# Gated linear attention into a gated state-space block: two of ten moves per group become ScalarE copies, and one group's moves change places with loads in the queue

## The chip, the cores and the metric

The kernel runs on one core of a Trainium2 chip. The metric is the device time of one execution in microseconds. A second number, the span, is the time from the first to the last instruction that the hardware profiler recorded in one profiled execution; the execution's own time is a little longer than its span.

## The reference

Batch B = 4, heads H = 8, sequence S = 768, head size D = 48; the model width is H·D = 384, and the inner width of the second block is 512. All arrays are fp32 (two weights arrive in double precision and are converted on the chip).

```python
# first block, per batch and head
for t in range(S):
    state = alpha[t, :, None] * state + outer(k[t], v[t])     # D x D
    y[t] = q[t] @ state
# bridge: (B,H,S,D) -> (B,S,H*D)
x = y.transpose(0, 2, 1, 3).reshape(B, S, H * D)
# second block
val, gate = split(x @ w_in)                                    # 2 x 512 wide
for t in range(S):
    h = exp(A_log) * h + val[t]
    ys[t] = h
out = (silu(gate) * ys) @ w_out
```

## The kernel before, in words

Two programs stand in the kernel; `fast` runs, and `general` only if a check at the end finds inputs outside of what `fast` can treat. All that follows is `fast`.

**Tiling.** The work is cut into N = 12 groups of 256 time steps (three groups a batch), each of G = 2 chunks of C = 128. The first block runs in its chunked form: a running product of alpha scales q and k, `scores` makes 128 x 128 score tiles, `masks` keeps the causal half, `values` multiplies by v, `state` and `carried` bring in what came before the chunk. The result of a group is in two PSUM tiles `y[0]` and `y[1]`, each 128 x 2 x 256. Head h = 4s + 2e + i lies in tile i, column block e, on partitions 64s to 64s + 47; time runs along the free axis. So a head has its 48 channels on the partitions 0 to 47 or 64 to 111.

**The bridge.** The second block wants x transposed, xT: 384 channels on the partitions as three blocks (kk = 0, 1, 2) of 128, time along the free axis. Head h occupies the channels 48h to 48h + 47. `join` evicts `y[1]` and `y[0]` with one ScalarE activation each (lines 727 and 728) into `y_sb`, and then `transfers` moves each head with a DMA from `y_sb` to its rows of xT (line 738); heads 2 and 5 cross a border of two blocks and take two moves, so that a group takes ten. Heads 0 and 4 go to the rows 0 of block 0 and 64 of block 1, which are also the partitions that they come from.

**The second block.** `project(n, cc)` makes for each cc of NI = 4 blocks of 128 inner channels the two products pv and pg (line 754), kk = 0, 1, 2 in turn for each, from xT and the weights. `hidden` runs the recurrence as a scan on VectorE (line 762); `gate` takes Silu of pg on ScalarE (line 773) and multiplies on GpSimd (line 774); in group 0 it multiplies on VectorE (line 770), with Silu at line 906. `output` multiplies by w_out (line 787) and stores.

**Weights.** They come as double precision bit patterns and are put together by `low_word` (ScalarE, line 512), `high_word` (VectorE, lines 526 and 528) and `word_sum` (GpSimd, line 535), in between the first groups' work. The first pv of group 0 needs the first of these sums.

**Order.** The program runs under a manual schedule: each engine executes its instructions in the order in which the code writes them, and the framework adds only the waits. SP issues almost all DMAs in one queue. Completion semaphores of DMAs are reused in turn, eight for SP's and eight for GpSimd's: a DMA's issue waits until the one eight earlier of that kind has landed. Groups 0, 1 and 2 load alpha, k and q in natural layout (`pair`, line 421) and transpose them on TensorE (`natural_alpha`, line 577; `natural_qk`, line 596); from group 3 on they come in another layout (`loads`, line 406) and VectorE transposes them (line 619). The start of the program is written out by hand. There, group 0's moves are issued by GpSimd, and all later groups' by SP:

```python
    join(0, nc.gpsimd)()
    ...
    join(1, SP)()
    load_v(2, SP)
    for cc in range(NI):
        pv, pg = project(0, cc)
```

In SP's queue the loads of alpha, k and q of group 2 stand after the weights, then the ten moves of group 1, then v of group 2, then the loads of group 3. From group 2 on, the block for n in 1..N-1 interleaves group n's second block with group n + 1's first; its `attend` ends with `join(m, SP)()`, and the next round's `block(n, 0)` reads that xT.

Of the kernel before, what the change touches and what calls it, by code (L numbers as in the profile page):

```python
# [13 lines left out]
AF = mybir.ActivationFunctionType  # L14
# [332 lines left out]
def fast(  # L347
# [18 lines left out]
    nc = tc.nc  # L366
    B, H, S, D = q.shape
    DM = H * D
    DI = moe_A_log.shape[0]
    C = 128  # L370
# [47 lines left out]
    def load_natural(name, m, c, engine):  # L418
        b, g = divmod(m, NG)
        src = {"a": alpha, "q": q, "k": k}[name]  # L420
        engine.dma_start(out=natural(name, m)[:, c, :, 0:D],  # L421
                         in_=src[b, :, ds(g * GC + c * C, C), :].rearrange("h p d -> p h d"))
# [4 lines left out]
    def load_v(m, engine, cs=range(G)):  # L427
        b, g = divmod(m, NG)
        for c in cs:
            engine.dma_start(out=vs[m % NV][:, c, :, 0:D],  # L430
                             in_=v[b, :, ds(g * GC + c * C, C), :].rearrange("h p d -> p h d"))
# [14 lines left out]
    def load_w_out(i, engine):  # L446
        engine.dma_start(out=bits_out[:, ds(2 * i, 2)].rearrange("p cc n two -> p cc (n two)"),
                         in_=moe_w_out.bitcast(U32)[ds(2 * C * i, 2 * C)].rearrange("(cc p) n -> p cc n", p=C))
# [251 lines left out]
    def carried(m, c):  # L700
        ch = (m % NG) * G + c
        if not ch:
            return
        for e in range(2):
            for s in range(2):
                for i in range(2):
                    p, rows = 2 * s + e, ds(64 * i, D)
                    nc.tensor.matmul(ys[m][i][ds(64 * s, D), e, ds(c * C, C)], S_sbs[ch - 1][rows, p, :],  # L708
                                     Zs[m][rows, p, 0, ds(c * C, C)], start=False, stop=True,
                                     skip_group_check=True)  # L710
# [12 lines left out]
    def join(m, engine):  # L723

        y = ys.pop(m)
        y_sb = p2.tile([C, 4, GC], FP32, tag="y_sb", name="y_sb")
        nc.scalar.activation(y_sb[:, 1::2], y[1], AF.Copy)
        nc.scalar.activation(y_sb[:, 0::2], y[0], AF.Copy)
        xT = xTs[m] = p2.tile([C, NK, GC], FP32, tag="xT", name="xT")

        def transfers():
            for h in range(H):
                s, a = divmod(h, 4)
                d = 0
                while d < D:
                    kk, row = divmod(h * D + d, C)
                    size = min(D - d, C - row)
                    engine.dma_start(out=xT[ds(row, size), kk], in_=y_sb[ds(64 * s + d, size), a])  # L738
                    d += size
        return transfers  # L740
# [54 lines left out]
    SP, ACT = nc.sync, nc.scalar  # L795
# [5 lines left out]
    def pair(name, m, one, other):  # L801
        load_natural(name, m, 0, one)
        load_natural(name, m, 1, other)
# [31 lines left out]
    k_times, q_times = natural_qk(0, "k"), natural_qk(0, "q")  # L835
    for i in range(2):
        load_w_out(i, SP)
    for name in "akq":
        pair(name, 2, SP, SP)

    warm(2)
    evict = natural_alpha(1)
# [21 lines left out]
    state(0, 1)  # L864
    carried(0, 1)
    join(0, nc.gpsimd)()
    k_times, q_times = natural_qk(1, "k"), natural_qk(1, "q", ps_mm)
    warm(2)
# [30 lines left out]
    carried(1, 0)  # L899
    carried(1, 1)  # L900
    join(1, SP)()
    load_v(2, SP)
    for cc in range(NI):
        pv, pg = project(0, cc)
# [15 lines left out]
    for n in range(1, N):  # L920
# [8 lines left out]
        def attend():  # L929
            if att:  # L930
                state(m, 0)
                values(m, 0)
                values(m, 1)
                state(m, 1)
                carried(m, 0)
                carried(m, 1)
                join(m, SP)()
# [49 lines left out]
@with_exitstack  # L987
def kernel(ctx: ExitStack, tc: tile.TileContext, *args):
    with tc.manual_schedule():
        good = fast(tc, *args)  # L990
    with tc.If(good <= 0):
        general(tc, *args)
# [30 lines left out]
```

## Time and profile before

| | us |
|---|---|
| median of 4 runs | 304.48 (302.75 to 305.66) |
| the profiled execution's own time | 303.63 |
| its span | 301.9 |
| TensorE busy (PE) | 287.3 |
| TensorE weight loads (PEld), beside PE | 227.2 |
| VectorE busy (DVE) | 226.2 |
| GpSimd busy (POOL) | 106.8 |
| ScalarE busy (ACT) | 95.1 |
| DMA, mean rate over the span | 143 GB/s |

The profile is one execution. Engines run side by side, so their busy times don't add up to the span. A releaser, written after an arrow, is what ended an idle time, inferred from semaphores. "SPq" is SP issuing a DMA, and the time of such a row covers the issue, with any holding back by full queues, not the transfer; a chain entry "DMA xT<-y_sb" is from issue to landing. Times written as moments are from the span's start.

### The profile page before, as it was taken

The page shows a single profiled execution, that of the slowest core. Times are in us where ns is not written, and L with a number is a line of the kernel's source. Part 1 is how long each engine was busy: PE and PEld are TensorE (multiplying, and loading weights), DVE is VectorE, ACT ScalarE, POOL GpSimd, SP SyncE. Part 2 cuts the span into 40 slices and gives each one's busy share as a digit, 9 for nine tenths or more (in the row PEclk, how much of TensorE's full clock was granted, in tenths as well). Part 3 has the DMA queues.
Part 4 walks back from the last instruction along what each step waited for, and adds up shares of the span by engine and source line. Part 5 has one row for each costly group of instructions (what it writes and reads, how often), then busy time and mean ns, then how long its engine had stood idle before and what let it go on. Part 6 is the DMA issues. An engine that isn't in the chain of part 4 may idle for free.

```text
span 301.9 us, 6124 instructions
## 1 busy us (share of the span) xinstructions
PE 287.3 (95%) x2347; PEld 227.2 (75%) x2347; DVE 226.2 (75%) x263; ACT 95.1 (32%) x198; POOL 106.8 (35%) x107
## 2 busy tenths in 40 slices
PE   7899699999999999999999999999999999999990
PEld 3497486887687787787887887886886886885860
DVE  5999398789899399699699699699699695302200
ACT  4264234151521521421531521521531531321111
POOL 6035843053352243262333333452423523411110
PEclk9999889999999999999999999999999999999998
DMA  9999995999398694695693595793693401101101
GB/s 131 163 191 322 321 148 108 230 269 201 105 237 133 166 230 70 166 224 83 182 219 67 140 226 86 189 210 67 179 216 66 106 9 46 52 21 35 52 7 59
DMA packets 72782, 43.26 MB, mean 143 GB/s; under 512 B 47876, under 2 KB 72104, under 8 KB 72744
## 3 DMA queue, kind: packets, MB, share of 16 engines
q1 hardware_dynamic: 71376, 42.19, 68.4%
q8 instruction: 20, 0.33, 0.5%
q0 software_dynamic: 320, 0.39, 0.5%
q10 hardware_dynamic: 1048, 0.20, 0.4%
q14 instruction: 18, 0.15, 0.2%
HBM read 33.33 MB, written 4.72 MB: 126 GB/s over the span
## 4 chain that ended last, share of the span: by engine, by line
PE 86%; DMA 7%; SPq 3%; ACT 1%; issue 1%; ACTq 0%
PE pv L754 22%; PE pg L754 21%; PE o L787 19%; PE sc L674 7%; PE y L697 7%; DMA xT<-y_sb 5%; PE st L718 3%; PE y L708 3%; PE tp L664 2%; DMA raw_q<-in_q_dram 2%; SPq L738 2%; SPq L421 1%; PE warm L823 1%; PE tn L596 1%; PE tn L577 1%
## 5 line engine op out<-in xcount | busy, mean ns | idle before, releaser
L774 POOL TENSOR_TENSOR f<-sg,hh 128x256 f32<-128x256 f32 x44 | 57.1, 1298 | 104.7 <-ACT sg L773 65.3
L754 PE MATMUL pv<-xT,w_in 128*128 128x256 f32 x288 | 73.4, 390 | 3.2 <-DMA xT<-y_sb 3.2
L754 PE MATMUL pg<-xT,w_in 128*128 128x256 f32 x288 | 71.2, 384 | 0.0
L787 PE MATMUL o<-w_out,f 128*128 128x384 f32 x192 | 64.1, 487 | 0.0
L754 PEld LDWEIGHTS pv<-xT,w_in 128*128 128x128 f32 x288 | 53.0, 191 | 14.1 <-issue 3.5
L754 PEld LDWEIGHTS pg<-xT,w_in 128*128 128x128 f32 x288 | 55.5, 193 | 8.2 <-DVE hh L762 0.5
L787 PEld LDWEIGHTS o<-w_out,f 128*128 128x128 f32 x192 | 36.4, 190 | 22.9 <-DVE hh L762 0.2
L685 POOL TENSOR_TENSOR A<-A,mask 128x512 f32<-128x512 f32 x22 | 27.5, 1271 | 67.0 <-ACT A L684 67.0
L773 ACT ACTIVATE sg<-pg 128x256 f32<-128x256 f32 x44 | 16.9, 383 | 93.7 <-PE pg L754 93.7
L762 DVE TENSOR_TENSOR_SCAN hh<-a_dec,hh,pv 128x256 f32<-128x256 f32 x32 | 23.3, 728 | 27.1 <-PE pv L754 25.2
L628 DVE TENSOR_TENSOR_SCAN prod<-aT,first 128x1024 f32<-128x1024 f32 x12 | 32.4, 2700 | 0.1
L640 DVE TENSOR_TENSOR_SCAN inv<-aT,last 128x1025 f32<-128x1025 f32 x12 | 30.1, 2507 | 0.4
L686 DVE TENSOR_TENSOR A<-sc,mask 128x512 f32<-128x512 f32 x22 | 15.0, 689 | 19.4 <-PE sc L674 19.3
L791 ACT ACTIVATE o_sb<-o 128x384 f32<-128x384 f32 x24 | 11.8, 490 | 50.8 <-PE o L787 46.5
L674 PEld LDWEIGHTS sc<-Z 48*128 48x128 f32 x384 | 22.4, 188 | 3.2 <-issue 2.4
L674 PE MATMUL sc<-Z 48*128 48x128 f32 x384 | 24.7, 279 | 0.0
L697 PE MATMUL y<-A,v 128*64 128x128 f32 x384 | 23.5, 274 | 0.0
L697 PEld LDWEIGHTS y<-A,v 128*64 128x64 f32 x384 | 20.7, 137 | 0.4 <-DVE A L686 0.3
L619 DVE STREAM_TRANSPOSE aT<-raw_a 128x1024 f32<-128x1024 f32 x9 | 18.4, 2040 | 0.0
L619 DVE STREAM_TRANSPOSE Z<-raw_q 128x1024 f32<-128x1024 f32 x9 | 18.2, 2022 | 0.0
L619 DVE STREAM_TRANSPOSE Z<-raw_k 128x1024 f32<-128x1024 f32 x9 | 18.2, 2020 | 0.0
L762 DVE TENSOR_TENSOR_SCAN hh<-a_dec,pv 128x256 f32<-128x256 f32 x16 | 10.7, 667 | 7.2 <-PE pv L754 7.2
(93 smaller groups left out, 262.8 us busy)
## 6 DMA issues: line engine op xcount, KB each, us to landing
raw_k<-in_k_dram SPq DMA_DIRECT2D x24, 192.0 KB, 5.5
raw_q<-in_q_dram SPq DMA_DIRECT2D x24, 192.0 KB, 6.3
v<-in_v_dram SPq DMA_DIRECT2D x24, 192.0 KB, 6.6
out_dram<-o_sb SPq DMA_DIRECT2D x24, 192.0 KB, 1.9
raw_a<-in_alpha_dram SPq DMA_DIRECT2D x23, 192.0 KB, 4.1
xT<-y_sb SPq DMA_DIRECT2D x66, 48.0 KB, 2.0
raw_a<-in_alpha_dram SPq DMA_DIRECT2D x18, 176.0 KB, 4.2
raw_k<-in_k_dram SPq DMA_DIRECT2D x18, 176.0 KB, 5.8
```

The lines of the kernel that those rows point to most:

```text
L619: nc.vector.transpose(out=to.rearrange("p h (c j) -> p h j c", j=NT), in_=raw_bufs[m % NR][name].rearrange("p h (j d) -> p h j d", d=D)[:, ...
L628: nc.vector.tensor_tensor_scan(out=prod, data0=aT[:, 0:4 * GC], data1=first.rearrange("p h n -> p (h n)"), initial=0.0, op0=ALU.mult, op1= ...
L640: nc.vector.tensor_tensor_scan(out=inv[:, ::-1], data0=aT[:, ::-1], data1=last.rearrange("p h n -> p (h n)")[:, 0:4 * GC + 1][:, ::-1], in ...
L674: nc.tensor.matmul(sc[i][:, p, :], Z[rows, p, 1, cols], Z[rows, p, 0, cols], start=True, stop=True)
L685: nc.gpsimd.tensor_mul(A[:, 1], A[:, 1], mb)
L686: nc.vector.tensor_mul(A[:, 0], sc[0], mb)
L697: nc.tensor.matmul(ys[m][i][ds(64 * s, 64), e, ds(c * C, C)], v_sb[:, c, 2 * p + i, :], A[:, i, p, :], start=(c == 0 and e == 0), stop=Fal ...
L754: nc.tensor.matmul(pj, w_in[cc][:, kk, vg, :], xT[:, kk, :], start=(kk == 0), stop=(kk == NK - 1))
L762: nc.vector.tensor_tensor_scan(out=hh, data0=a_dec[:, cc:cc + 1].to_broadcast([C, GC]), data1=pv, initial=prev_h[cc][:, GC - 1:GC] if n % ...
L773: nc.scalar.activation(sg, pg, AF.Silu)
L774: nc.gpsimd.tensor_mul(fs[n][:, cc, :], sg, hh)
L787: nc.tensor.matmul(os[c], fs[n][:, cc, ds(c * C, C)], w_out[:, cc, :], start=(cc == 0), stop=(cc == NI - 1))
```

## The change

`join` no longer copies all of y[0] to `y_sb`. It copies the half that holds heads 2 and 6, and writes heads 0 and 4 with two ScalarE activations of 48 x 256 from PSUM straight to their rows of xT; the moves are then eight. The order on ScalarE is: y[1] to `y_sb`, half of y[0] to `y_sb`, head 0, head 4. Each move waits only for the eviction that it reads, so the first one of a group (head 1 now) waits for y[1] alone. Apart from that, the four loads of k and q of group 2 leave their place ahead of group 1's moves in SP's queue and stand behind them.

```diff
@@ join
         nc.scalar.activation(y_sb[:, 1::2], y[1], AF.Copy)
-        nc.scalar.activation(y_sb[:, 0::2], y[0], AF.Copy)
+        nc.scalar.activation(y_sb[:, 2], y[0][:, 1], AF.Copy)
         xT = xTs[m] = p2.tile([C, NK, GC], FP32, tag="xT", name="xT")
 
         def transfers():
             for h in range(H):
                 s, a = divmod(h, 4)
+                if not a:
+                    kk, row = divmod(h * D, C)
+                    nc.scalar.activation(xT[ds(row, D), kk], y[0][ds(64 * s, D), 0], AF.Copy)
+                    continue
                 d = 0
                 while d < D:
...
     for i in range(2):
         load_w_out(i, SP)
-    for name in "akq":
-        pair(name, 2, SP, SP)
+    pair("a", 2, SP, SP)
...
     join(1, SP)()
+    for name in "kq":
+        pair(name, 2, SP, SP)
     load_v(2, SP)
```

GpSimd's instructions lose two moves in group 0 and keep their order otherwise; SP's lose two moves in each of the eleven later groups; TensorE's and VectorE's are the same, in the same order.

## The prediction

> **What bounds the kernel now.** I read the engines' shares first, then the chain that ended last, then the timeline wherever the chain leaves the tensor engine.
>
> ```profile
> PE 287.3 (95%) x2347; PEld 227.2 (75%) x2347; DVE 226.2 (75%) x263; ACT 95.1 (32%) x198; POOL 106.8 (35%) x107
> PE 86%; DMA 7%; SPq 3%; ACT 1%; issue 1%; ACTq 0%
> L754 PE MATMUL pv<-xT,w_in 128*128 128x256 f32 x288 | 73.4, 390 | 3.2 <-DMA xT<-y_sb 3.2
> ```
>
> TensorE is busy 95% of the span and carries 86% of the chain. From 96 us on the chain is TensorE and next to nothing else, some 22.3 us a group, so a gain of the tensor engine before that point stays to the end, and what is not TensorE's lies in front of it. Its only row with real idle time is pv (line 754), 3.2 us, all of it for the moves into xT. The chain in order of time shows where:
>
> ```profile
> 21.84 0.60 ACT y_sb L727
> 22.43 0.50 ACT y_sb L728
> 22.94 0.30 issue
> 23.23 6.75 DMA xT<-y_sb
> 29.98 0.28 issue
> 30.26 5.91 DMA xT<-y_sb
> 36.17 0.45 issue
> 36.62 1.19 PE pv L754 x2
> 37.82 2.25 PE pg L754 x6
> ...
> 78.69 3.32 DMA xT<-y_sb
> ```
>
> Columns are start, length, what. The chain passes through two xT moves of group 0 in a row, one released by the other. The timeline tells why, and what else hangs there:
>
> ```profile
> 30.26 1.02 POOL L738 DMA_DIRECT2D xT<-y_sb  x2 [2.62 <-DMA xT<-y_sb]
> 47.61 0.42 PEld L577 LDWEIGHTS tn<-ident,raw_a 128*128 128x128 f32 x4 [0.18 <-DVE f L770]
> 70.96 8.32 SPq L738 DMA_DIRECT2D xT<-y_sb  x10
> 82.15 0.67 PE L754 MATMUL pv<-xT,w_in 128*128 128x256 f32 x2 [0.52 <-DMA xT<-y_sb]
> ```
>
> GpSimd issues eight moves from 23.23 to 27.64 and then sits 2.62 us until the first has landed: moves nine and ten (heads 6 and 7) reuse the completion semaphores of the first two. They go out at 30.26 and 30.77 and land 5.9 and 5.8 us later, the last at 36.53; the eighth went out at 27.12 and landed 6.6 us later, at 33.70. The second place is group 2: pv begins at 80.50 and its last two matmuls wait until 82.15.
>
> ```profile
> 32.80:36.20 3.40, 1.11 (x4) 0.34 (x3) 0.50 (x1) 1.61 (x3) 3.40 (x5) 1.00 1.03 361
> 36.20:39.60 3.40, 2.98 (x7) 2.47 (x8) 1.71 (x4) 0.00 (x0) 0.84 (x1) 0.50 1.04 183
> 45.00:50.00 5.00, 5.00 (x26) 3.79 (x25) 3.81 (x11) 3.18 (x6) 2.87 (x3) 1.00 0.21 53
> 50.00:58.00 8.00, 8.00 (x39) 5.93 (x38) 6.30 (x6) 1.84 (x5) 0.67 (x1) 1.00 1.07 217
> ```
>
> Here the columns after the length are busy time of PE, PEld, DVE, ACT, POOL, then granted clock, DMA share, GB/s. TensorE has 1.11 us of work in 3.4 us while it waits, and runs the next 3.4 us at half clock. The DMA engines are nearly idle from 45 to 50 us and full (1.07 to 1.10) from 50 to 76.
>
> **What the skill says.** "TensorE: Matmul & The Clock Gate", Part 1 on the HAM clock gate: the clock is halved after an idle window of about 3.4 us, in free-running windows of 3413 ns. The trace agrees in length: half clock from 36.20 for 3.4 us. "DMA: Bandwidth & Descriptors", Queues, rings and completion order: each DMA engine takes turns, packet by packet, between the queues that have work for it. A POOL move takes 6.6 us beside the weight loads where an SP move in a quiet stretch takes 2.0, so the small moves share but do not overtake. "ScalarE: Activation LUTs", What ACT_TABLE_LOAD costs: an ACTIVATE with immediate operands takes 186 ns + 0.833 ns an element, less 93 ns back to back. For 512 elements that is an estimate of 0.61; the trace has 0.60.
>
> **Part one: eight moves a group, two ACT copies.**
>
> 1. ACT. Before: two evictions of 512 columns, 21.84 to 22.93. After: one of 512, then three of 256 (half of y0, heads 0 and 4). The 128x256 ACTIVATE of line 773 takes 383 ns, so about 0.3 each back to back: 0.60 + 0.9 = 1.5, that is 0.4 more a group. After the join ACT's next work in group 0 is line 512 at 24.77, which waits for a load: hidden by 1.4 us. In group 3 the evictions end at 91.28 and the next Silu (line 773) waits for pg until 92.99: hidden by 1.7. Cost nothing; with that cover gone 11 groups by 0.4, 4.4 us.
> 2. POOL's start. Its first move is now head 1, which needs only y1, done at 22.44, so it starts at about 22.74 instead of 23.23: 0.5 earlier.
> 3. POOL's end. Eight moves carry the same bytes as the first eight before, and no move waits for a landing. Issue ends at about 27.2, and the last lands at 33.70 - 0.5 = 33.2. Were the landing time set by the full DMA engines alone it would stay at 33.7; both ends are kept.
> 4. The weight sums of line 535 stand behind the moves on POOL: from 31.29 to about 27.2. Their inputs are there (DVE done 26.53, ACT 25.70). The first pv waits for nothing else.
> 5. TensorE. carried(1,1) still ends near 32.6. pv's kk = 0 and 1 take 4 x 0.215 = 0.86 (1.29 us for six), so kk = 2 starts at 33.46, after the landing at 33.2. Before it started at 36.62: 3.16 earlier (2.8 with the late bound).
> 6. Clock. The wait that emptied the window before 36.2 is gone, so it should stay full. pv's last two and pg took 1.19 + 2.25 = 3.44 where full clock takes 0.43 + 1.29 = 1.72: 1.72 more. Together 4.88 at the end of pg.
> 7. What is late next: DVE in that loop. Per block it does scan 0.68, four weight operations of 0.55, product 0.41, so 3.3 us against TensorE's 2.59. Before, first scan to third product ran 37.85 to 47.55 with 0.42 idle, so 9.28 of work. After: 33.95 + 9.28 = 43.23. The transposes tn at 47.61 already waited for it, and now go at 43.35 where TensorE alone would give 43.0. So 4.25 us arrive at 48, not 4.88.
>
> **Part two: k and q of group 2 behind xT of group 1 on SP.** SP waits before each transfer for the landing of the one eight earlier, and also for room: the second raw_a of group 2 is issued from 28.09 to 35.02. Then:
>
> 8. The eight xT(1) moves start at about 35.1 (y1 is ready at 33.93). The last two wait for the raw_a landings (39.62, 40.50), so they end at about 41.2 and land at about 43. TensorE reads xT(1) at 54.24 - 4.25 = 50.0. With ten moves in the old place the last lands near 50.8, with eight there about 49; so this step by itself frees little.
> 9. The four k and q transfers move from 35.12 to about 41.3. In an empty queue v takes 3.6 us from issue to landing and raw_a 4.9; I take 4.0: first k at 45.3, then 1.2 us each as before, the last q at 48.9. The transposes of line 596 need it at 56.83 - 4.25 = 52.6. Hidden with 3.7 us to spare.
> 10. Then v(2), and group 3's loads. Before, the hole in DMA lasted from q's landing at 45.05 to v's at 52.49; now there is a shorter one from 40.5 to 45.3. The v loads land at 50.1 and 51.3, the first raw_a of group 3 at 52.1 instead of 54.98: the full stream runs 2.9 us earlier. Bounds: 0 if the new hole is as long as the old, 4 if no hole is left.
> 11. xT(2), at the end of that stream. Before, the first move was held by full queues until 73.58 and the others followed at 0.63. The eighth was issued at 77.43; less 2.9 this is 74.5, and with 2.0 to 3.3 us to land 76.5 to 77.8. TensorE wants it at 80.50 + 0.86 - 4.25 = 77.1. I take 77.3. Gain at that point 82.15 - 77.3 = 4.8.
> 12. Later groups: the last xT(3) move lands at 101.58 and is read from 103.5, so moves saved there are worth nothing.
>
> Sum: 4.8 us off the profiled execution, whose own time is 303.63 (span 301.9 and 1.7 around it): 298.8. The median of the four runs is 0.85 higher, 304.48, which gives 299.7. The clock's windows run free, and in other runs the same wait may empty two of them, so I put it at 299.5.
>
> **Rivals.**
> - A, the forecast: 299.5, of which gains between 3.1 and 7 us count.
> - B, the full DMA stretch takes it back. For it: DMA share 1.07 to 1.10 from 50 to 76, and xT(2) stands behind v(3). If step 10 brings nothing, xT(2) is only 1.26 earlier by its two moves, pv's kk = 2 starts at 80.9, and the gain is 1.3 us: 303.2; with half of step 10, 301.7. Against it: the DMA share of 0.21 between 45 and 50. I take 302.5.
> - C, slower: k and q of group 2 come too late. They now wait behind eight moves which wait for the slowest loads (raw_a took 12.4 us to land). Each us after 52.6 is one us of TensorE; the gain is gone when q lands after 57.4, which is 8.5 us past my estimate. A landing at 61.5 gives 304.5 - 4.8 + 8.9 = 308.6. Against it: from 41 us the queue is empty, and nothing in the trace takes 16 us from issue to landing.
> - D, the copies don't spare the wait because something else holds pv: then step 7's DVE loop or ACT's copies decide, and the time stays near 304. Against it: in step 4 every input is there by 29.2.
>
> **Numbers.** A 0.72, B 0.17, C 0.05, D 0.06. A measurement of this kernel can tell about 1% (3.0 us) from no change. A is faster by over 1%, and a third of B's spread comes over that line too, which I count as 0.04. Faster 0.76, same 0.19, slower 0.05. The range takes in the late bounds of steps 10 and 11 and half of B at the top, and a second half-clock window in the median run at the bottom: 297.4 to 302.4.
>
> **What would show it.** Right: POOL's moves without a wait and its line-535 sums at 27; pv without a pause after 33.5 and no half clock after 36; tn (line 577) near 43.4; k and q landed by 49; xT(2)'s last move at 77 to 78. Wrong: pv's last pair waiting beyond 34.5 (step 3), line 596 waiting for raw_k or raw_q (step 9), pv of group 2 waiting until 79 or more (step 10).

## The result and the profile after

The changed kernel has a median of 302.41 us (37 runs, 299.7 to 305.85) against 303.64 for the kernel before (58 runs): ratio 0.9937, 95% interval 0.992 to 0.9954. The medians are of all runs; the ratios, here and below, leave out runs more than 1.5% above the fastest of the same kernel, among them one of 1033.66 us of the fix without the change. That is about 1.9 us by the ratio (1.2 by the medians), where 5.0 were forecast (299.5, range 297.4 to 302.4, against a median of 304.48). The profiled execution took 302.82, with a span of 301.1.

The page's shares, the chain's and the row of pv, which was TensorE's only one with real idle time before:

```profile
PE 287.3 (95%) x2347; PEld 227.0 (75%) x2347; DVE 226.2 (75%) x263; ACT 100.4 (33%) x222; POOL 104.5 (35%) x105
PE 87%; DVE 4%; SPq 3%; DMA 2%; issue 1%; ACT 1%; ACTq 0%
L758 PE MATMUL pv<-xT,w_in 128*128 128x256 f32 x288 | 73.2, 389 | 3.3 <-DMA xT<-y_sb 3.3
```

The wait for xT did not go: 3.3 us, as before 3.2. It has moved. The timeline of the start (columns: start, length, engine, line, what, count, idle time before and its releaser):

```profile
22.71 4.22 POOL L742 DMA_DIRECT2D xT<-y_sb  x8 [2.83 <-ACT y_sb L728]
26.99 1.97 POOL L535 TENSOR_TENSOR w_in<-w_in,wr 128x384 int32<-128x384 int32 x2
32.51 1.56 PE L758 MATMUL pv<-xT,w_in 128*128 128x256 f32 x6
43.35 0.42 PEld L577 LDWEIGHTS tn<-ident,raw_a 128*128 128x128 f32 x4 [0.52 <-DVE f L774]
```

GpSimd issues eight moves without a stop, the weight sums follow at 26.99, the first pv runs all six matmuls through, and tn (the transposes of group 2's alpha) starts at 43.35, where before it was 47.61. `block(1, 0)` starts at 49.97 instead of 54.24: TensorE is 4.27 us ahead. The same view from 65 us on, around the moves of group 2:

```profile
65.58 0.60 ACT L727 ACTIVATE y_sb<-y 128x512 f32<-128x512 f32 x1 [2.50 <-PE y L708]
70.31 9.13 SPq L742 DMA_DIRECT2D xT<-y_sb  x8
77.72 0.67 PE L758 MATMUL pv<-xT,w_in 128*128 128x256 f32 x2 [1.43 <-DMA xT<-y_sb]
78.92 0.67 PE L758 MATMUL pv<-xT,w_in 128*128 128x256 f32 x2 [0.52 <-DMA xT<-y_sb]
80.97 1.19 PE L758 MATMUL pv<-xT,w_in 128*128 128x256 f32 x2 [1.38 <-DMA xT<-y_sb]
```

All three pairs of group 2's pv wait, 3.33 us together, and the last goes at 80.97, only 1.18 ahead of before (82.15). SP needs 9.13 us for eight moves, where ten took 8.32. It also comes to them late. The first eviction of group 2's y ends at 66.2, and SP issues the first move at 70.31. The transfer eight earlier in SP's order, whose completion semaphore that move takes over, is the third load of k of group 4; it landed at 70.23. So a wait of the kind that the change removes from GpSimd's moves now stands in front of SP's. In the kernel before, y was evicted only at 70.94, and its first move went at 70.96. The busy times by stretch show the rest (after the length: PE, PEld, DVE, ACT, POOL, then granted clock, DMA share, GB/s):

```profile
41.00:45.00 4.00, 3.89 (x21) 2.80 (x20) 3.25 (x7) 2.08 (x5) 2.21 (x3) 1.00 0.38 84
45.00:50.00 5.00, 5.00 (x17) 3.01 (x16) 4.46 (x6) 1.70 (x4) 0.00 (x0) 1.00 1.10 161
76.90:80.50 3.60, 1.34 (x4) 0.59 (x4) 0.76 (x2) 0.26 (x1) 2.34 (x2) 1.00 0.22 55
80.50:83.90 3.40, 2.93 (x7) 2.42 (x8) 1.70 (x2) 0.00 (x0) 0.00 (x0) 0.51 0.93 263
```

The half clock that stood at 36.2 to 39.6 now stands at 80.5 to 83.9, after a window with 1.34 us of TensorE work in 3.6; in the chain the last pair and pg take 1.19 + 2.25 = 3.44 us where before they took 0.67 + 1.29 = 1.96. At pg's end the changed kernel stands at 84.41, the kernel before at 84.11. So in these two executions the whole gain is given back in one place: from 4.27 ahead to 1.18 ahead by waiting, 3.09 us, and from there to 0.30 behind by the clock, 1.48. The 1.9 us are an average over executions: those of the changed kernel with a mean granted clock of 0.996 or more took 299.7 to 301.4 us, those at 0.990 to 0.993 mostly 301.8 to 303.5, so half clock in the middle of the program seems not to come in every one. Where it falls in each is not shown. After that both run the same, and TensorE's last product is done 0.3 us later than before. The span is nevertheless 0.8 shorter, because the issue of the last store took SP 0.33 instead of 1.52; nothing in the change accounts for that.

The DMA hole lies at 41 to 45 us now (share 0.38), where it was at 45 to 50 (0.21). The loads of group 3 begin to land at 53.85 (54.98 before), and v of group 3, right ahead of group 2's moves in the queue, lands at 76.13 (76.30 before).

### The profile page after: what moved, and what is told of

Same layout as the page of the kernel before. It is cut to its first block, busy times and chain, and to the rows that moved or that the text cites. A ratio compares the mean times of both kernels' runs of the same rounds, so it can differ in the third digit from the quotient of the medians.

```text
span 301.1 us, 6112 instructions
## 1 busy us (share of the span) xinstructions
PE 287.3 (95%) x2347; PEld 227.0 (75%) x2347; DVE 226.2 (75%) x263; ACT 100.4 (33%) x222; POOL 104.5 (35%) x105
## 4 chain that ended last, share of the span: by engine, by line
PE 87%; DVE 4%; SPq 3%; DMA 2%; issue 1%; ACT 1%; ACTq 0%
PE o L791 21%; PE pv L758 21%; PE pg L758 19%; PE y L697 7%; PE sc L674 7%; PE st L718 4%; PE y L708 3%; PE tp L664 2%; DMA raw_q<-in_q_dram 2%; PE tn L596 1%; SPq L742 1%; SPq L421 1%; PE warm L827 1%; DVE bank L526 1%; DVE Z L602 1%
## 5 line engine op out<-in xcount | busy, mean ns | idle before, releaser
L778 POOL TENSOR_TENSOR f<-sg,hh 128x256 f32<-128x256 f32 x44 | 55.8, 1268 | 110.6 <-ACT sg L777 70.9
L718 PEld LDWEIGHTS st<-v,ktm 128*64 128x64 f32 x320 | 11.4, 137 | 3.9 <-issue 3.3
```

The costliest lines, as they stand in the source:

```text
L718: nc.tensor.matmul(st[ds(64 * i, 64), p, :], ktms[c][:, p, i, :], vs[m % NV][:, c, 2 * p + i, 0:D], start=(ch == 0 and p == 0), stop=(ch = ...
L778: nc.gpsimd.tensor_mul(fs[n][:, cc, :], sg, hh)
```

## The experiments

All are compared with the kernel before on the same chip. "The fix" below is the edit of the third experiment (k and q of group 4 behind group 2's moves).

**Part one alone.** k and q of group 2 back in their old place:

```diff
-    pair("a", 2, SP, SP)
+    for name in "akq":
+        pair(name, 2, SP, SP)
...
-    for name in "kq":
-        pair(name, 2, SP, SP)
```

> Part one alone: eight moves and two copies, k and q of group 2 back ahead of group 1's moves. Theory (full DMA queue decides at xT of group 2): the first pv runs through as in the changed kernel and tn of group 2 starts near 43.4, but the loads of group 3 start only about 1.2 us earlier than in the kernel before, so pv of group 2 waits as in the changed kernel: ratio to before 0.994, within 0.002 of the changed kernel. Rival (the new order is what serves group 1, xT of group 1 is late without it): pv of group 1 waits at 50 us by 1 us or more, and the ratio is 0.998 or more.

Measured: 0.9951 (0.9926 to 0.9975), median 301.63; the interval takes in the changed kernel's ratio of 0.9937. `block(1, 0)` starts at 49.83 without a wait: group 1's last move is down at 48.87, so part two was not needed there. The hole stays where it was in the kernel before (busy times by stretch):

```profile
41.00:45.00 4.00, 3.89 (x20) 2.83 (x19) 3.11 (x7) 2.09 (x4) 2.09 (x3) 1.00 1.01 121
45.00:50.00 5.00, 5.00 (x17) 2.99 (x17) 4.60 (x6) 1.70 (x5) 0.00 (x0) 1.00 0.39 86
```

and group 2's pv waits as in the changed kernel (timeline):

```profile
80.07 1.19 PE L758 MATMUL pv<-xT,w_in 128*128 128x256 f32 x2 [1.37 <-DMA xT<-y_sb]
```

Group 3's first load lands at 53.24, 0.6 earlier than with part two, and the last pair of group 2's pv goes at 80.07, 0.9 earlier. No gain from part two shows and, in these two profiles, it costs a little.

**Part two alone.** On the kernel before:

```diff
-    for name in "akq":
-        pair(name, 2, SP, SP)
+    pair("a", 2, SP, SP)
...
     join(1, SP)()
+    for name in "kq":
+        pair(name, 2, SP, SP)
```

> Part two alone: ten moves and no copies, k and q of group 2 behind group 1's moves. Theory: GpSimd's wait and the half clock at 36 us stay, group 1's xT comes earlier than anyone needs it, the hole in the DMA traffic only moves from 45-50 to 41-46 us, and xT of group 2 lands where it did: ratio 1.000, within 0.002. Rival (the order by itself frees the full stretch, as step 10 of the prediction had it): ratio 0.996 or less, with pv of group 2 no longer waiting.

Measured: 1.0031 (1.0009 to 1.0054). The same was expected; it is a little slower. Ten moves keep SP until 45.04, the loads of k and q follow, and group 3's first load lands at 57.93, 3 us later than before. The stretch in which the DMA engines are nearly idle meanwhile:

```profile
41.00:45.00 4.00, 4.00 (x19) 3.43 (x18) 3.02 (x7) 1.18 (x2) 2.40 (x3) 0.94 0.20 49
```

In the timeline GpSimd still stops after eight moves, and group 2's moves take SP 9.84 us and are waited for longer than before (there 0.52):

```profile
30.59 1.00 POOL L738 DMA_DIRECT2D xT<-y_sb  x2 [2.44 <-DMA xT<-y_sb]
71.97 9.84 SPq L738 DMA_DIRECT2D xT<-y_sb  x10
83.33 0.67 PE L754 MATMUL pv<-xT,w_in 128*128 128x256 f32 x2 [1.19 <-DMA xT<-y_sb]
```

The order has the opposite sign of step 10 of the prediction: it makes the full stretch start later, not earlier.

**The place of group 2's moves in the queue.** The changed kernel, with k and q of group 4 issued behind group 2's moves:

```diff
-        if n + 3 < N:
+        if n == 1:
+            load_raw("a", n + 3, [SP])
+        elif n + 3 < N:
             loads(n + 3)
...
             go(1)
             attend()
+            for name in "kq":
+                load_raw(name, n + 3, [SP])
             go(1)
```

> The changed kernel, and in addition the loads of k and q of group 4 issued behind group 2's xT moves instead of ahead of them (round n = 1 only). Theory: eight loads of 0.8 us each leave the queue ahead of xT of group 2, its last move lands by 74 to 75 us, pv of group 2 starts at about 76.3 without a wait and at full clock, 5 us ahead of the kernel before, and it stays so: ratio 0.984, about 298.6 us. Rival (the total of the traffic decides and not the place in the queue): k or q of group 4 or xT of group 3 is then late instead, and the ratio stays at 0.990 or above.

Measured: 0.984 (0.982 to 0.9859), median 298.2, as the theory had it. The row of pv on the page:

```profile
L758 PE MATMUL pv<-xT,w_in 128*128 128x256 f32 x288 | 72.3, 387 | 0.0
```

The timeline around group 2's moves:

```profile
66.43 5.16 SPq L742 DMA_DIRECT2D xT<-y_sb  x8
71.70 1.93 SPq L406 DMA_DIRECT2D raw_k<-in_k_dram  x4
76.45 1.56 PE L758 MATMUL pv<-xT,w_in 128*128 128x256 f32 x6
```

And the stretch that ran at half clock in the changed kernel:

```profile
80.50:83.90 3.40, 3.40 (x53) 2.96 (x53) 3.33 (x5) 0.71 (x2) 2.36 (x2) 1.00 1.10 266
```

pv has no idle time left, SP comes to the eight moves at 66.43, as soon as y is evicted, and they take 5.16 us instead of 9.13; group 2's pv goes through at 76.45, and the clock stays full. k and q of group 4 land later, the last at 81.02, and nobody misses them: VectorE takes up k at 85.25 and q at 89.10. This shows where the gain of the change was: behind eight loads in SP's queue.

**The same in every round.** k and q of group n + 3 always behind the moves:

```diff
         if n + 3 < N:
-            loads(n + 3)
+            load_raw("a", n + 3, [SP])
...
                 join(m, SP)()
+            if n + 3 < N:
+                for name in "kq":
+                    load_raw(name, n + 3, [SP])
```

> As the one before, but in every round the loads of k and q stand behind the xT moves. Theory: group 2 as there; it differs only if xT of group 3 is late there (its last move lands near 98 to 99 and is wanted at 99): then up to 1 us better, else the same, ratio 0.983 to 0.984. Rival: the loads, issued some 10 us later in each round, come late for VectorE's transposes, and the ratio is above 0.990.

Measured: 0.9837 (0.9818 to 0.9857). No difference from the third experiment shows; one round was all.

**The fix without the change.** The two hunks of the third experiment on the kernel before:

```diff
+        if n == 1:
+            load_raw("a", n + 3, [SP])
...
+            for name in "kq":
+                load_raw(name, n + 3, [SP])
```

> The kernel before (ten moves, no copies, k and q of group 2 in the old place), with only k and q of group 4 behind group 2's moves. Theory (two gates in a row, GpSimd's ninth and tenth move first, the full queue in front of xT of group 2 second): the second gate alone held the kernel before for 0.8 us, so ratio 0.997, and the wait for group 0's xT and the half clock at 36 us stay. Rival (the place of the k and q loads is worth the 5 us by itself): 0.986 or less.

Measured: 1.0 (0.9977 to 1.0022). The 0.8 us expected lie just outside of the interval, so nothing is shown of them; the 5 us of the rival are excluded. Group 2's xT is no longer waited for (its pv runs six matmuls through from 79.58), but the gate ahead of it is still closed (timeline):

```profile
30.38 0.51 POOL L738 DMA_DIRECT2D xT<-y_sb  x1 [2.23 <-DMA xT<-y_sb]
36.76 0.67 PE L754 MATMUL pv<-xT,w_in 128*128 128x256 f32 x2 [2.13 <-DMA xT<-y_sb]
```

The stretch with that wait, cut where the clock's windows lie in this execution (see the last section), and the stretch after it:

```profile
34.79:38.20 3.41, 1.44 (x7) 1.32 (x8) 0.74 (x2) 0.11 (x1) 2.61 (x3) 1.00 1.16 304
36.90:40.30 3.40, 3.40 (x17) 2.99 (x18) 2.77 (x6) 1.17 (x2) 0.74 (x2) 1.00 1.06 170
```

The two gates stand in a row: the fix alone is worth 0.0%, the change alone 0.6%, both together 1.6%. In this execution the clock stayed full after the wait (1.00): its gap is a little shorter, and the window with most of it still holds 1.44 us of work, where in the kernel before it held 1.12.

**The fix with part one alone.** The first experiment's edit, with the fix:

```diff
+    for name in "akq":
+        pair(name, 2, SP, SP)
...
+            for name in "kq":
+                load_raw(name, n + 3, [SP])
```

> Eight moves and k and q of group 4 behind group 2's moves, but k and q of group 2 in their old place ahead of group 1's moves. Theory (part two of the change serves nothing): group 1's last move lands near 49, TensorE wants it at 50, no wait, ratio 0.984 as with part two. Rival (with the second gate open part two is needed): pv of group 1 or group 3's loads come late, ratio 0.987 or more.

Measured: 0.984 (0.9793 to 0.9887), median 298.36. With the second gate open too, no gain from part two shows, within an interval of half a per cent to each side.

**Nine moves.** The version with the fix, and head 4 of group 0 by a move:

```diff
+        if not m:
+            nc.scalar.activation(y_sb[ds(64, D), 0], y[0][ds(64, D), 0], AF.Copy)
...
-                if not a:
+                if not a and (m or not s):
```

> The version with k and q of group 4 behind, but head 4 of group 0 goes by a move again, so that GpSimd has nine moves in that one group. Theory (the reuse of a completion semaphore is the cost, not the copies or the bytes): the ninth is issued only when the first has landed, near 29.5, lands near 35.3, pv's last pair goes at 35.4 instead of 33.5; loss 1.9 us, and up to 1.7 more if the clock's window falls on the gap: ratio 0.989 to 0.995. Rival (each move less is worth the same, 0.5 us of issue): loss 0.5 us, ratio 0.986.

Measured: 0.992 (0.9895 to 0.9945), as the theory had it. One move more costs 0.8% against the version without it (timeline):

```profile
23.24 4.39 POOL L744 DMA_DIRECT2D xT<-y_sb  x8 [2.82 <-ACT y_sb L728]
30.00 0.50 POOL L744 DMA_DIRECT2D xT<-y_sb  x1 [2.36 <-DMA xT<-y_sb]
35.96 0.70 PE L760 MATMUL pv<-xT,w_in 128*128 128x256 f32 x2 [1.79 <-DMA xT<-y_sb]
```

The ninth goes out at 30.00, after the landing of the first at 29.72, and lands 5.9 us later. What the change bought at the start is the issue without a wait: the rival, 0.5 us for each move less, would have given 0.986.

**Fewer bytes ahead of group 2's moves.** The changed kernel without the loads of q of group 4 (that q is left out):

```diff
-        if n + 3 < N:
+        if n == 1:
+            for name in "ak":
+                load_raw(name, n + 3, [SP])
+        elif n + 3 < N:
             loads(n + 3)
```

> The changed kernel without the four loads of q of group 4 (that group's q is left out; old contents of the buffer are used). All else keeps its place. Theory (what stands in the queue ahead of xT of group 2 is carried at the DMA engines' full rate, 0.8 us a load): its moves land 3.2 us earlier, the last at 77.6 instead of 80.8, pv's last pair is late by about 0.5, the half clock mostly gone: ratio 0.985 to 0.989. Rival (the moves are held by something of their own, as the time of their issue on SP): they land within 1 us of the changed kernel, ratio 0.992 or more.

Measured: 0.983 (0.9781 to 0.9879); the gain is larger than expected, though the interval reaches into the expected range. The first move lands at 72.74 instead of 76.30, 3.6 us earlier for four loads; but the seven behind it also follow faster, and the eighth is issued at 74.09 instead of 78.85 (timeline):

```profile
66.74 7.94 SPq L742 DMA_DIRECT2D xT<-y_sb  x8
76.76 1.56 PE L758 MATMUL pv<-xT,w_in 128*128 128x256 f32 x6
```

So it is the loads ahead in the queue, and their total is not needed as an explanation of its own: taking four of them away and putting eight behind give the same time.

**Filling the hole.** Part one alone, with v of group 2 ahead of group 1's moves:

```diff
-    join(1, SP)()
     load_v(2, SP)
+    join(1, SP)()
```

> Eight moves, k and q of group 2 in the old place, and v of group 2 also ahead of group 1's moves (nothing else is changed; group 4's loads stay ahead of group 2's moves). Theory (an idle stretch of the DMA engines while SP issues small moves is what sets the start of the full stretch, step 10 of the prediction in another place): v fills some 2 us of that hole, group 3's loads start about 1 us earlier than with v behind, xT of group 2 lands 1 to 2 us earlier, ratio 0.988 to 0.992; group 1's last move lands near 50, at the edge of being late. Rival (the full stretch ends where it ends): xT of group 2 within 0.5 us of where it was with v behind (79.9), ratio 0.994 to 0.996.

Measured: 0.9895 (0.9874 to 0.9916). The ratio is inside the theory's range, but the trace doesn't bear out its reason. The hole:

```profile
45.00:50.00 5.00, 5.00 (x18) 2.99 (x17) 4.51 (x6) 1.70 (x5) 0.00 (x0) 1.00 0.39 85
```

and the pairs of pv that wait, of group 1 and of group 2:

```profile
51.45 0.67 PE L758 MATMUL pv<-xT,w_in 128*128 128x256 f32 x2 [0.67 <-DMA xT<-y_sb]
79.46 0.67 PE L758 MATMUL pv<-xT,w_in 128*128 128x256 f32 x2 [0.64 <-DMA xT<-y_sb]
```

The hole at 45 to 50 is as wide as in the first experiment (0.39), and group 3's first load lands at 53.17 instead of 53.24, where the theory wanted 1 us. Group 2's xT is complete at 79.33 instead of 79.94, 0.6 earlier: between the rival (within 0.5) and the theory (1 to 2), and nearer to the rival. The other part is the clock: 0.67 us of waiting now falls at 51 us, less is left at 77, the emptiest window there still holds 2.40 us of work, and the last pair takes 0.67 instead of 1.19. Its pg then runs at full clock too. So in this execution the result is the half-clock window's more than the hole's; what the other runs owe to it is not shown.

## Why the prediction was wrong

**Steps 1 to 7 held.** The evictions end at 23.33 and nobody waits for them. GpSimd starts at 22.71 (22.74 forecast), the eighth move lands at 32.93 (33.2), pv's six go through from 32.51, the clock stays full there, tn starts at 43.35 (43.35). VectorE's loop as the next bound (step 7) is in the chain: DVE has 4% of it, where before it had no share. The nine-move run shows that the ninth move's wait for the landing of the first was the cost.

**Step 8 was mis-sized, and with it step 9.** I gave the first xT(1) move 0.6 us of issue. At 35 us the move was held, for want of room in the queue as I read it, like raw_k in the same place before (3.42 us):

```profile
L742 SPq DMA_DIRECT2D xT<-y_sb x1: 3150/3150/3150, 35.0 to 35.0; - x1
```

The eight moves end at 42.70 instead of 41.2, and k of group 2 goes out at 42.81 instead of 41.3. These 1.5 us are most of the 1.75 by which group 3's first load lands later than forecast (53.85 instead of 52.1). The last q lands at 50.51 (48.9 forecast), still ahead of its use at 53.2, so the slower rival C did not come.

**Step 10 failed, and this step decided the result.** It let the full stretch start 2.9 us earlier and end 2.9 us earlier. It started 1.1 earlier, by the two moves less and not by the order, as part two alone shows (3 us later), and it ended 0.2 earlier. While SP issues eight small moves no loads are issued; the order only shifts that hole from 45-50 to 41-45 us. Why a stretch that starts 1.1 us earlier (1.7 with part one alone) then ends 0.2 (0.9) earlier is not settled; in the trace of the changed kernel most of the difference arises at the two stores of group 0, which land 1.6 us after the load ahead of them instead of 0.5.

**Step 11 carried the error on and added one.** The eighth xT(2) move was to be issued at 74.5 and went at 78.85: 2.9 us for the stretch whose end did not move, 0.4 because the first move is accepted later than before, and 1.0 because the fourth is held for 1.58, for which no cause was found. Its landing then took 2.0. pv's last pair was to go at 77.3 and went at 80.97, 3.7 us late, and the empty window before it halved the clock, for 1.5 more. The half clock at this place stood in no step. Yet the prediction held what was needed: the Trainium skill, "TensorE: Matmul & The Clock Gate", Part 1 on the HAM clock gate, says that an idle window halves the clock. The trace had shown at 36 us that the window need not be wholly idle (1.12 us of work in it), and the window from 77.14 to 80.55, with 1.34 us of work, did the same.

**The rivals.** B named the mechanism that came, and the place; it had 0.17. It was priced at 302.5, 0.9935 of the median shown then; 0.9937 was measured. That the numbers are so close is in part luck. B gave its gain to the two moves less, but the eighth move went at 78.85, no earlier than the tenth before (78.69); the last pair came 1.2 us earlier because the last landing took 1.98 us instead of 3.32. And B's sum has no half clock in it. The argument against it, the idle share of 0.21 between 45 and 50, was wrong: the hole stands while SP issues the small moves, and reordering only shifted it (part two alone) or left it as wide (v ahead), so it was no reserve. D is excluded by the timeline of the start. The forecast's own time was not out of reach: the version that puts eight loads behind the moves ran at 298.2.

**Point by point of "what would show it".** Right: no wait in GpSimd's moves, sums at 27, no pause at 33.5, no half clock at 36, tn at 43.4. Wrong: q landed at 50.5 and not by 49, and pv of group 2 waited beyond 79, which was named as the sign against step 10.

## What to carry to other kernels

When a wait at the front goes, follow what it had hidden to the next transfer that the freed engine wants, and ask what stands ahead of it in its queue: here 4.3 us were lost behind eight loads that nobody used until some 18 us after they had landed. Putting those behind the urgent moves was worth 1.0% on top of the change's 0.6%, and nothing without the change. Ask also whose completion semaphore the urgent transfer takes over, for it can't be issued before that one has landed. In a queue that is in order, small urgent moves belong ahead of bulk loads with slack; a full queue also holds the issue of the small ones. And charge a stall of TensorE that can leave less than about 1.4 us of work in a 3.4 us clock window (last section) with a possible half-clock stretch on top, here 1.5 us.

## What of the hardware was not expected

- A move of 48 KB is held in its issue on SP as long as a load of 192 KB in the same place: 3.15 us in the changed kernel, 3.42 in the kernel before and 3.13 in part one alone, at 34 to 35 us. For the first move of group 2 the traces show what it is held for: in all nine in which it is held, its issue ends 0.13 to 0.30 us after the load four places ahead of it in SP's order has landed (landing at 73.85, end at 74.01 in the changed kernel).
- Ten moves at 0.63 us each keep SP from issuing loads for over 6 us, and the DMA engines run nearly dry in that time (share 0.20 to 0.39 over 4 to 5 us in the kernel before, the changed kernel and each part alone), although the next loads need nothing but their turn: with v of group 2 ahead of the moves its issue starts at 41.52 instead of 47.59.
- How empty a window must be for half clock can be read off. In each trace the changes of the granted clock lie whole multiples of 3.413 us apart (before: half clock begins at 36.20 and again at 299.03, 77 times 3.413 later), which gives the windows of that execution. TensorE's work in the windows ahead of a half-clock stretch in the middle of the program was 0.94 us (part one alone), 1.12 (before), 1.14 (part two alone) and 1.34 (changed kernel). Windows with 1.44 (the fix without the change), 1.97 (nine moves) and 2.40 (v ahead) were followed by full clock. So here the border lies between 1.34 and 1.44 us of work in 3.413, and nearly the same wait costs a half-clock stretch or none.
